# Retention and mixture kernel: the first two blocks' retention placed ahead of the slots, and a lead of two chunks

## The chip, the cores and the metric

The kernel runs on one core of one Trainium2 chip. The metric is the device time of one execution in microseconds (us), as the median of several runs.

## What is computed

Three stages follow one another. Each takes the output of the one before.

```python
scores = scale * np.matmul(q, k.transpose(0, 1, 3, 2))      # 4 batches, 8 heads, 576 tokens, 64 wide
ret = scores * Dmat                                          # gamma_h ** (i - j) for j <= i, else 0
x = np.matmul(ret, v)                                        # then 2304 tokens x 512
h = x @ w_in;  g = h * np.cos(h);  x = g @ w_out             # 512 -> 2048 -> 512
h = x @ w_in2; g = where(h >= 1, h, where(h <= -1, 0, (h + 1) ** 2 / 4)); out = g @ w_out2
```

The first stage is called retention here, the second layer 0, the third layer 1. The weights arrive as 64-bit floats.

## The kernel before

**Tiles and blocks.** The 2304 tokens are cut into five blocks, block 0 of 256 tokens and blocks 1 to 4 of 512. The hidden width of 2048 is cut into 16 chunks c of 128. A slot (l, c) is block l times chunk c of layer 0: a first matmul group (`mm1`, 12 matmuls: three products of split operands, four pieces of the inner dimension), an activation chain on ACT, DVE and POOL (`actA`, `actB`, `actC`), and a second group (`mm2`, 12 matmuls) that runs LAG = 2 slots later and sums into PSUM banks: S and O for block 0, y0 to y3 for the blocks of 512. After chunk 15 `evac` copies these banks out.

**Order of slots.** The list `slots` (L338) sets the order by hand: block 0 leads block 1 by LEAD = 3 chunks, so it runs (0,0), (0,1), (0,2), (0,3), (1,0), (0,4), (1,1) and so on; then blocks 2 to 4 follow, one after the other. While block 0 and block 1 run, each weight chunk is loaded as raw bits (`load_raw`; chunks from 4 on twice, the second time shifted into `rsh`), converted on ACT and DVE into two single-precision halves (`begin`, `convert`), used at once, and the first layer's chunk is also written to DRAM (`make_wi1`) for later blocks. The converted wi tiles live in a pool of LEAD + 2 = 5 buffers.

**Retention.** It works on chunks of up to 128 tokens (`Chunk`), two in block 0, five in block 1, four or five in each other block. Their steps: `load` (q and k, then k and v, then a table of scalings), `prep` (v scaled on DVE, L271), `scores` (L279, into two PSUM banks), `masked` (two maskings on DVE, L285), `full` (state products, L301, and the product with the running state T, L296), `inner` (L309), `state` (T updated, L320 or L322), `post` (scaled out of PSUM by DVE, L327, then split into two parts by ACT, L334, and DVE, L335, into the block's input `xhl`). The tile that holds one chunk's q, k and v comes from pool `ap`, of two buffers. Block 0's chunks are done ahead of the slots. The chunks of the later blocks are spread over a window of slots of the block before (`window`, `mk`, `run_plan`); block 1's over slots 0 to 4, on the banks y2, y3 and y0, y1; block 2's over the last three slots of block 1, on S and O.

**Queues.** Each engine runs its instructions in order, and nearly all DMAs are issued by SP's queue in order. A scheduler of the framework shifts neighbouring instructions within the data's dependences, so the order on an engine is not quite that of the code.

**After that.** While blocks 2 to 4 run, layer 1's weights are converted in the background (`bg`, from the slot behind (0,15) on) and layer 1 then runs as seven products per pair of chunks (`product`, `group`).

Of the kernel before, what the change touches and what calls it, by code (L numbers as in the profile page):

```python
# [7 lines left out]
F32 = mybir.dt.float32  # L8
# [10 lines left out]
B, H, S, D = 4, 8, 576, 64  # L19
NT, DM, DFF = B * S, H * D, 2048  # L20
P = 128
# [11 lines left out]
SEQ = {p: k for k, (p, _, _) in enumerate(PRODS)}  # L33
LAG2 = 3
LAG = 2
LEAD = 3
TWICE = 4
MAGIC = 1.5 * 2.0 ** 23
INV2PI = 0.15915494309189535
# [26 lines left out]
def retention_moe_kernel(ctx: ExitStack, tc: tile.TileContext, qk, kv, win1, wout1, win2, wout2, mask, vtab, ptab, out):  # L66
# [2 lines left out]

    const = ctx.enter_context(tc.tile_pool(name="const", bufs=1))  # L70
    wp = ctx.enter_context(tc.tile_pool(name="wp", bufs=1))
    wr = ctx.enter_context(tc.tile_pool(name="wr", bufs=LEAD + 2))
    xp = ctx.enter_context(tc.tile_pool(name="xp", bufs=5))
    ap = ctx.enter_context(tc.tile_pool(name="ap", bufs=2))
    act = ctx.enter_context(tc.tile_pool(name="act", bufs=2))
# [36 lines left out]
    def load_raw(L, i, c, late=False):  # L112
        src = wsrc[L, i][c]
        twice = L == 0 and c >= TWICE
        tag = "raw" if twice else ("raw", "rsh")[turn[0] % 2] if L == 0 else ("raw", "raw", "rsh")[turn[0] % 3]
        turn[0] += not twice and not late
        t = wp.tile([P, DM, 2], I32, tag="wo0", name="raw") if late else cv.tile([P, DM, 2], I32, tag=tag, name="raw")
        i0 = SY.dma_start(out=t, in_=src)
        if L == 1 and len(done) > 1 and not late:
            behind(i0, done[-2])  # L120
        t2 = None
        if twice:
            t2 = cv.tile([P, 4 * DM + 8], I16, tag="rsh", name="rsh")
            SY.dma_start(out=t2[:, 1:1 + 4 * DM], in_=src.rearrange("p n two -> p (n two)").bitcast(I16))
        raws[L, i, c] = t, t2
# [113 lines left out]
    CH = {}  # L239
# [8 lines left out]
    class Chunk:  # L248
# [6 lines left out]
            self.first, self.last = self.t == 0, self.t + self.n == S  # L255
            self.banks = banks

        def load(self, other=None):
            n = self.n
            both = ap.tile([P, 4, DM], F32, tag="qkv", name="qkv")  # L260
            self.qk = both[:, 0:2].rearrange("p a (i m) -> p a i m", i=NP)
            self.kv = both[:, 2:4]
            SY.dma_start(out=self.qk, in_=qk[self.i])
            (other or SY).dma_start(out=self.kv[:n], in_=kv[self.i][:n])
            self.pt = ap.tile([P, NP, P], F32, tag="pt", name="pt")
            (other or SY).dma_start(out=self.pt[:, :, :n], in_=ptab[:, :, self.t:self.t + n])
# [294 lines left out]
    for i, (b, t, n) in enumerate(CHUNKS):  # L561
        members.setdefault(_block_of(b * S + t), []).append(i)

    window = {1: (0, LEAD + 1)}
    b1_end = pos_of[1, NC - 1]
    window[2] = (b1_end - LEAD + 1, b1_end + 1)
    for l in range(3, NBLK):
        window[l] = (pos_of[l - 1, 0] + 1, pos_of[l - 1, NC - 1] - 1)
    ends = {}
    for l in range(1, NBLK):  # L570
        s0, s1 = window[l]
        span = 2 * (s1 - s0) / len(members[l])
        for k, i in enumerate(members[l]):
            g = int(2 * s0 + k * span)
            e = int(2 * s0 + (k + 1) * span) - 1
            e = max(e, g)
            pos = [g, g + (e - g) // 3, e]
            ends[i] = e
            gl_ = max(g - 9, ends.get(i - 2, -99))
            banks = ("S", "O") if l > 1 else (("y2", "y3"), ("y0", "y1"))[k % 2]  # L580

            def mk(i=i, g=g, pos=pos, gl_=gl_, banks=banks):
                def ld():
                    CH[i] = Chunk(i, banks)
                    CH[i].load()
                at(gl_, ld)
                at(g - 1, lambda: CH[i].prep())
                at(pos[0], lambda: CH[i].scores())
                at(pos[0], lambda: CH[i].masked())
                at(pos[1], lambda: CH[i].full())  # L590
                at(pos[1], lambda: CH[i].inner())
                at(pos[1], lambda: CH[i].state())
                at(pos[2], lambda: CH[i].post())
            mk()

    first = members[0]
    V.memset(half, 0.5)
    A.activation(half, half, AF.Sin)
    V.memset(half, 0.5)
# [6 lines left out]
    def warm(n, after=None):  # L606
        for _ in range(n):
            m = PE.matmul(wt[:, 0:P], wz, wz, start=True, stop=True)
            if after is not None:
                behind(m, after)  # L610
    warm(20)
    for k, i in enumerate(first):
        CH[i] = Chunk(i, (("S", "O"), ("y0", "y1"))[k])
        if i == 0:
            A.dma_start(out=vtb, in_=vtab)
            CH[i].load(A)
            A.dma_start(out=msk, in_=mask)
            load_raw(0, 0, 0)
        else:
            CH[i].load()  # L620
    load_raw(0, 1, 0)
    load_raw(0, 0, 1)
    for i in first:
        c = CH[i]
        c.prep()
        c.scores()
        c.masked()
        warm(10, c.lastpe)
        c.full()
        c.inner()  # L630
        c.state()
        warm(10, c.lastpe)
        c.post()
        if i == 0:
            make_wi1(0, begin(0, 0, 0))
    for p in range(-9, 0):
        run_plan(p)


    jobs = {}  # L640
    for c in range(NC):
        if c >= 1:
            jobs.setdefault(max(0, pos_of[0, c - 1]), []).append((0, c))
        jobs.setdefault(pos_of[0, c], []).append((1, c))
    order = [x for q in sorted(jobs) for x in jobs[q]]
    loaded = [(0, 0), (1, 0), (0, 1)]
    queue = [x for x in order if x not in loaded]
    load_raw(0, *queue.pop(0))

# [153 lines left out]
```

## Time and profile before

| | us |
|---|---|
| median of 3 runs | 918.56 (918.26 to 927.11) |
| profiled execution | 917.86 |
| its span, first to last instruction | 916.1 |
| PE busy in the span | 879.1 (96%) |
| DVE busy | 628.6 (69%) |
| ACT busy | 475.0 (52%) |

PE is TensorE's matmuls, PEld its weight loads, DVE is VectorE, ACT ScalarE, POOL GpSimd, SP the engine that issues the DMAs. A matmul is pipelined, so its duration in a row is longer than the distance to the next one's start; the distance is its cost. A row that merges several instructions (x24) bears the name and shape of the first. The granted clock is a share of the full 2.4 GHz: 1.00 or 0.50, or a mean over a stretch.

### The profile page before, as it was taken

Reading aid. Unit: us, or ns where it says so; the run is one execution under the profiler, and the core shown is the slowest. Engines: PE = TensorE matmul, PEld = TensorE weight load, DVE = VectorE, ACT = ScalarE, POOL = GpSimd, SP = SyncE. Lnnn points to the kernel's source line nnn. Section 1 sums busy time; section 2 is a strip of 40 time slices with the busy share of each in tenths; the row PEclk is TensorE's granted clock in tenths of the full one; section 3 lists DMA queues with packets and bytes.
Section 4 is the critical chain, followed back from the end, with each engine's and each line's share of the span. In section 5 each row is a group of like instructions: output and inputs, shape, how many; then the busy total and the mean of one; then the engine's idle time right before and its main releaser. Section 6 shows DMA issues by size and latency. Waiting matters only on the chain.

```text
span 916.1 us, 13560 instructions
## 1 busy us (share of the span) xinstructions
PE 879.1 (96%) x4876; PEld 754.2 (82%) x4876; DVE 628.6 (69%) x1155; ACT 475.0 (52%) x885; POOL 114.7 (13%) x84
## 2 busy tenths in 40 slices
PE   6788999999999999999999999999999999999997
PEld 6677887877778788788888878998888889889896
DVE  6987898358785967966888776456854546555454
ACT  3447888743655665565767653334433334433332
POOL 0022332203112221212222200000000000000000
PEclk8878999998999999999999999999999999999999
DMA  9998897138858667865686896666685656665531
GB/s 349 295 323 279 313 330 277 47 117 290 329 196 326 239 220 281 260 214 217 231 313 235 296 346 220 185 192 174 207 270 180 188 172 205 226 210 166 168 92 70
DMA packets 78115, 211.81 MB, mean 231 GB/s; under 512 B 9696, under 2 KB 21728, under 8 KB 78048
## 3 DMA queue, kind: packets, MB, share of 16 engines
q1 hardware_dynamic: 77088, 210.01, 67.7%
q10 hardware_dynamic: 960, 0.93, 0.3%
q8 instruction: 39, 0.64, 0.3%
q14 instruction: 28, 0.23, 0.1%
HBM read 170.02 MB, written 40.89 MB: 230 GB/s over the span
## 4 chain that ended last, share of the span: by engine, by line
PE 72%; DMA 12%; DVE 10%; ACT 3%; issue 2%; SPq 0%; DVEq 0%; ACTq 0%
PE hq L490 17%; PE h L359 15%; DMA raw<-in_wout_dram 5%; PE bky L374 5%; PE bky L375 4%; PE bky L542 4%; PE bky L376 4%; PE bky L543 4%; PE bky L544 4%; DMA q<-yd 2%; DMA qkv<-in_kv_dram 2%; DMA wi<-wd 1%; DVE W L142 1%; PE bkO L544 1%; PE bkS L543 1%
## 5 line engine op out<-in xcount | busy, mean ns | idle before, releaser
L490 PE MATMUL hq<-xc,wq 128*128 128x384 f32 x1008 | 199.8, 338 | 4.3 <-ACT sX L505 3.1
L359 PE MATMUL h<-xhl,wi 128*128 128x512 f32 (+1 forms) x864 | 196.7, 377 | 3.7 <-ACT xhl L334 3.0
L490 PEld LDWEIGHTS hq<-xc,wq 128*128 128x128 f32 x1008 | 180.2, 188 | 17.2 <-ACT sX L505 3.9
L359 PEld LDWEIGHTS h<-xhl,wi 128*128 128x128 f32 x864 | 153.1, 194 | 33.4 <-ACT xhl L334 3.4
L422 POOL TENSOR_TENSOR gl<-t,gh 128x512 fp32r<-128x512 f32 (+1 forms) x80 | 114.5, 1438 | 415.5 <-ACT gh L421 391.4
L421 ACT ACTIVATE gh<-t 128x384 fp32r<-128x384 f32 (+2 forms) x176 | 96.5, 549 | 58.2 <-DVE t L429 29.3
L524 ACT ACTIVATE t<-t,half 128x384 f32<-128x384 f32 x96 | 58.9, 616 | 112.4 <-DVE t L523 112.3
L374 PE MATMUL bky<-gh,wo 128*128 128x512 f32 x256 | 102.9, 402 | 5.6 <-ACT gh L421 5.5
L375 PE MATMUL bky<-gh,wo 128*128 128x512 f32 x256 | 101.5, 397 | 0.0
L376 PE MATMUL bky<-gl,wo 128*128 128x512 f32 x256 | 88.7, 392 | 0.0
L525 DVE TENSOR_TENSOR t<-t,sC 128x384 f32<-128x384 f32 x96 | 53.2, 556 | 34.7 <-ACT t L524 34.7
L542 PE MATMUL bky<-wo,gh 128*128 128x512 f32 x192 | 75.7, 394 | 0.9 <-ACT gh L421 0.9
L543 PE MATMUL bky<-wo,gh 128*128 128x512 f32 x192 | 75.5, 393 | 0.0
L414 ACT ACTIVATE t<-t 128x512 f32<-128x512 f32 (+1 forms) x80 | 46.3, 586 | 51.2 <-DVE t L409 51.0
L422 DVE TENSOR_TENSOR gl<-t,gh 128x384 fp32r<-128x384 f32 x96 | 53.1, 553 | 18.9 <-ACT gh L421 18.6
L523 DVE TENSOR_SCALAR t<-sC 128x384 f32<-128x384 f32 x96 | 34.1, 357 | 44.9 <-ACT sC L510 43.4
L374 PEld LDWEIGHTS bky<-gh,wo 128*128 128x128 f32 x256 | 48.6, 190 | 18.0 <-ACT gh L421 7.2
L544 PE MATMUL bky<-wo,gl 128*128 128x512 f32 x192 | 61.2, 394 | 0.0
L375 PEld LDWEIGHTS bky<-gh,wo 128*128 128x128 f32 x256 | 48.8, 191 | 9.9 <-issue 0.3
L141 DVE TENSOR_SCALAR X<-X 128x512 int32<-128x512 int32 x64 | 30.1, 470 | 36.4 <-ACT X L134 36.2
L376 PEld LDWEIGHTS bky<-gl,wo 128*128 128x128 f32 x256 | 47.3, 188 | 9.5 <-issue 0.2
L134 ACT ACTIVATE X<-raw 128x512 f32<-128x512 f32 x64 | 42.6, 666 | 21.7 <-DMA raw<-in_wout_dram 9.9
(126 smaller groups left out, 1376.8 us busy)
## 6 DMA issues: line engine op xcount, KB each, us to landing
wq<-wq SPq DMA_DIRECT2D x72, 512.0 KB, 4.0
wi<-wd SPq DMA_DIRECT2D x48, 512.0 KB, 5.1
wo<-wd SPq DMA_DIRECT2D x48, 512.0 KB, 4.6
raw<-in_win_dram SPq DMA_DIRECT2D x32, 512.0 KB, 5.4
raw<-in_wout_dram SPq DMA_DIRECT2D x32, 512.0 KB, 5.2
qkv<-in_qk_dram SPq DMA_DIRECT2D x20, 512.0 KB, 4.8
wd<-wi SPq DMA_DIRECT2D x16, 512.0 KB, 4.0
wq<-tw SPq DMA_DIRECT2D x32, 256.0 KB, 4.0
```

Source lines behind the costliest of these rows:

```text
L359: PE.matmul(hp[s][:, :n], w[:, a, kb, :], x[b][:, kb, :], start=(i == 0), stop=(i == 3 * KB - 1))
L374: PE.matmul(o, w[:, 0, es], a, start=first and e % per == 0, stop=False, skip_group_check=True)
L375: PE.matmul(o, w[:, 1, es], a, start=False, stop=False, skip_group_check=True)
L376: PE.matmul(o, w[:, 0, es], b, start=False, stop=last, skip_group_check=True)
L421: A.activation(a, u, AF.Copy)
L422: eng.tensor_tensor(out=b, in0=u, in1=f(a), op=ALU.subtract)
L490: PE.matmul(o, w[:, a, kb, :], x[b][:, kb, :], start=first and i == 0, stop=i == 5, skip_group_check=True)
L524: A.activation(t, t, AF.Square, scale=0.5, bias=half)
L525: V.tensor_tensor(out=t, in0=t, in1=h, op=ALU.max)
L542: PE.matmul(y, a[:, js], w[:, 0, :], start=n == 0, stop=False)
L543: PE.matmul(y, a[:, js], w[:, 1, :], start=False, stop=False)
L544: PE.matmul(y, b[:, js], w[:, 0, :], start=False, stop=n == NC - 1)
```

## The change

LEAD goes from 3 to 2, and the wi pool keeps its five buffers (LEAD + 3). All seven chunks of blocks 0 and 1 are put ahead of the slots in one list `first`; each is loaded three chunks ahead, on three pairs of banks in turn, and every other one takes its q, k, v tile from pool `xp` and not from `ap`. The first raw weights are loaded between these chunk loads, and wi 0, wo 0 and wi 1 are converted between the chunks. Chunk c's wi is begun three slots ahead of (0,c), before it was at (0,c-1). Block 2's window has two slots, not three, and its third and fourth chunk use y0 to y3. The diff, whole:

```diff
--- before.py
+++ after.py
@@ -33,7 +33,7 @@
 SEQ = {p: k for k, (p, _, _) in enumerate(PRODS)}
 LAG2 = 3
 LAG = 2
-LEAD = 3
+LEAD = 2
 TWICE = 4
 MAGIC = 1.5 * 2.0 ** 23
 INV2PI = 0.15915494309189535
@@ -69,7 +69,7 @@
 
     const = ctx.enter_context(tc.tile_pool(name="const", bufs=1))
     wp = ctx.enter_context(tc.tile_pool(name="wp", bufs=1))
-    wr = ctx.enter_context(tc.tile_pool(name="wr", bufs=LEAD + 2))
+    wr = ctx.enter_context(tc.tile_pool(name="wr", bufs=LEAD + 3))
     xp = ctx.enter_context(tc.tile_pool(name="xp", bufs=5))
     ap = ctx.enter_context(tc.tile_pool(name="ap", bufs=2))
     act = ctx.enter_context(tc.tile_pool(name="act", bufs=2))
@@ -255,9 +255,9 @@
             self.first, self.last = self.t == 0, self.t + self.n == S
             self.banks = banks
 
-        def load(self, other=None):
+        def load(self, other=None, pool=None):
             n = self.n
-            both = ap.tile([P, 4, DM], F32, tag="qkv", name="qkv")
+            both = (pool or ap).tile([P, 4, DM], F32, tag="x" if pool else "qkv", name="qkv")
             self.qk = both[:, 0:2].rearrange("p a (i m) -> p a i m", i=NP)
             self.kv = both[:, 2:4]
             SY.dma_start(out=self.qk, in_=qk[self.i])
@@ -561,13 +561,12 @@
     for i, (b, t, n) in enumerate(CHUNKS):
         members.setdefault(_block_of(b * S + t), []).append(i)
 
-    window = {1: (0, LEAD + 1)}
     b1_end = pos_of[1, NC - 1]
-    window[2] = (b1_end - LEAD + 1, b1_end + 1)
+    window = {2: (b1_end - LEAD + 1, b1_end + 1)}
     for l in range(3, NBLK):
         window[l] = (pos_of[l - 1, 0] + 1, pos_of[l - 1, NC - 1] - 1)
     ends = {}
-    for l in range(1, NBLK):
+    for l in range(2, NBLK):
         s0, s1 = window[l]
         span = 2 * (s1 - s0) / len(members[l])
         for k, i in enumerate(members[l]):
@@ -577,7 +576,8 @@
             pos = [g, g + (e - g) // 3, e]
             ends[i] = e
             gl_ = max(g - 9, ends.get(i - 2, -99))
-            banks = ("S", "O") if l > 1 else (("y2", "y3"), ("y0", "y1"))[k % 2]
+
+            banks = (("S", "O"), ("y0", "y1"), ("y2", "y3"))[max(0, k - 1) % 3 if l == 2 else 0]
 
             def mk(i=i, g=g, pos=pos, gl_=gl_, banks=banks):
                 def ld():
@@ -593,7 +593,7 @@
                 at(pos[2], lambda: CH[i].post())
             mk()
 
-    first = members[0]
+    first = members[0] + members[1]
     V.memset(half, 0.5)
     A.activation(half, half, AF.Sin)
     V.memset(half, 0.5)
@@ -609,41 +609,57 @@
             if after is not None:
                 behind(m, after)
     warm(20)
-    for k, i in enumerate(first):
-        CH[i] = Chunk(i, (("S", "O"), ("y0", "y1"))[k])
-        if i == 0:
+
+    def first_load(k):
+        i = first[k]
+        CH[i] = Chunk(i, (("S", "O"), ("y0", "y1"), ("y2", "y3"))[k % 3])
+        if k == 0:
             A.dma_start(out=vtb, in_=vtab)
             CH[i].load(A)
             A.dma_start(out=msk, in_=mask)
-            load_raw(0, 0, 0)
         else:
-            CH[i].load()
+            CH[i].load(pool=xp if k % 2 else None)
+
+    first_load(0)
+    first_load(1)
+    load_raw(0, 0, 0)
+    first_load(2)
     load_raw(0, 1, 0)
-    load_raw(0, 0, 1)
-    for i in first:
+    CH[first[0]].prep()
+    for k, i in enumerate(first):
         c = CH[i]
-        c.prep()
         c.scores()
         c.masked()
-        warm(10, c.lastpe)
+        if k < 2:
+            warm(10, c.lastpe)
+        if k + 1 < len(first):
+            CH[first[k + 1]].prep()
         c.full()
         c.inner()
         c.state()
-        warm(10, c.lastpe)
+        if k < 2:
+            warm(10, c.lastpe)
         c.post()
-        if i == 0:
+        if k + 3 < len(first):
+            first_load(k + 3)
+        if k == 2:
             make_wi1(0, begin(0, 0, 0))
+            load_raw(0, 0, 1)
+        if k == 4:
+            make_wo1(0, begin(0, 1, 0))
+            load_raw(0, 1, 1)
+    make_wi1(1, begin(0, 0, 1))
     for p in range(-9, 0):
         run_plan(p)
 
 
     jobs = {}
-    for c in range(NC):
-        if c >= 1:
-            jobs.setdefault(max(0, pos_of[0, c - 1]), []).append((0, c))
+    for c in range(1, NC):
+        if c > 1:
+            jobs.setdefault(max(0, pos_of[0, c] - 3), []).append((0, c))
         jobs.setdefault(pos_of[0, c], []).append((1, c))
     order = [x for q in sorted(jobs) for x in jobs[q]]
-    loaded = [(0, 0), (1, 0), (0, 1)]
+    loaded = [(1, 1)]
     queue = [x for x in order if x not in loaded]
     load_raw(0, *queue.pop(0))
```

Where this moves instructions, as they stand on the engines. First PE at the start of block 1's slots. bkS and bkO are block 0's sums, wo0 to wo3 its second-layer weights by chunk, xhl a block's input; h of 512 columns is block 1's. Before:

```order
L296 MATMUL bky3_662<-qkv_545,T_90 128x64 x4
L309 MATMUL bky3_662<-R_671,qkv_545 64x64 x8
L374 MATMUL bkS_645<-gh_784,wo3_726 128x256
L375 MATMUL bkS_645<-gh_784,wo3_726 128x256
...
L376 MATMUL bkO_646<-gl_785,wo3_726 128x256
L359 MATMUL h_770<-xhl_357,wi_237 128x512 x4
L359 MATMUL h_808<-xhl_231,wi_739 128x256 x12
```

And now:

```order
L296 MATMUL bkO_496<-qkv_410,T_90 128x64 x4
L309 MATMUL bkO_496<-R_505,qkv_410 64x64 x8
L374 MATMUL bkS_680<-gh_599,wo0_448 128x256
L375 MATMUL bkS_680<-gh_599,wo0_448 128x256
...
L374 MATMUL bkS_680<-gh_656,wo1_615 128x256
...
L376 MATMUL bkO_681<-gl_657,wo1_615 128x256
L359 MATMUL h_696<-xhl_346,wi_358 128x512 x4
L359 MATMUL h_750<-xhl_235,wi_626 128x256 x5
```

Behind block 1's last chunk of retention stood the second layer of (0,3), and those of (0,0) to (0,2) were done by then; now the first second-layer slots at all, (0,0) and (0,1), stand there, and (0,3)'s first layer comes with (1,0).

SP's queue around the first load for block 2 (qkv_1868 before, qkv_1918 now); raw and rsh are weights, wd their copies to DRAM, pt the scalings. Before:

```order
L263 DMA qkv_545<-in_qk_dram 128x1024
L264 DMA qkv_545<-in_kv_dram 64x1024
L266 DMA pt_548<-in_ptab_dram 128x4x64
L118 DMA raw_735<-in_win1_dram 128x1024
L263 DMA qkv_1868<-in_qk_dram 128x1024
L264 DMA qkv_1868<-in_kv_dram 128x1024
L124 DMA rsh_750<-in_wout1_dram 128x2048
L163 DMA wd0_0_4_96<-wi_739 128x1024
```

And now:

```order
L263 DMA qkv_350<-in_qk_dram 128x1024
L264 DMA qkv_350<-in_kv_dram 128x1024
L163 DMA wd0_0_2_94<-wi_571 128x1024
L266 DMA pt_353<-in_ptab_dram 128x4x128
L263 DMA qkv_1918<-in_qk_dram 128x1024
L264 DMA qkv_1918<-in_kv_dram 128x1024
L118 DMA raw_678<-in_wout1_dram 128x1024
L118 DMA raw_732<-in_win1_dram 128x1024
```

The load for block 2 came behind the raw load of wi 5; now the raw loads of wo 3 and wi 5 come behind it.

PE at the end of block 1, from the second layer of its last chunk (wo15) to block 2's first slot. Before:

```order
L309 MATMUL bkO_2249<-R_2258,qkv_2123 64x128 x8
...
L374 MATMUL bky0_901<-gh_2431,wo15_2018 128x512
...
L376 MATMUL bky0_901<-gl_2432,wo15_2018 128x512
L279 MATMUL bkO_2316<-qkv_2219 128x128 x4
L301 MATMUL bkS_2315<-qkv_2219 64x64 x8
```

And now:

```order
L376 MATMUL bky3_847<-gl_2410,wo15_2056 128x512
L279 MATMUL bky0_2264<-qkv_2163 128x128 x4
L279 MATMUL bky2_2323<-qkv_2232 128x128 x4
L279 MATMUL bky1_2265<-qkv_2163 128x128 x4
L279 MATMUL bky3_2324<-qkv_2232 128x128 x4
L296 MATMUL bky1_2265<-qkv_2163,T_90 128x128 x4
L309 MATMUL bky1_2265<-R_2274,qkv_2163 64x128 x8
L301 MATMUL bky2_2323<-qkv_2232 64x64 x8
L309 MATMUL bky3_2324<-R_2333,qkv_2232 64x128 x8
```

Of block 2's four chunks the third was complete on PE before the last second-layer slots of block 1, and the fourth began between them; now the third and the fourth begin behind them.

## Rows read from the trace of the kernel before

**Rows 1.** The windows of the whole core: us, each engine busy (instructions), clock, DMA.

```profile
12.00:68.00 56.00, 44.91 (x457) 39.27 (x458) 52.09 (x107) 25.47 (x54) 6.69 (x4) 0.80 0.96 325
67.00:100.00 33.00, 29.91 (x145) 25.49 (x146) 24.92 (x48) 23.21 (x50) 6.42 (x6) 0.86 0.85 302
100.00:160.00 60.00, 56.78 (x315) 48.97 (x314) 52.08 (x96) 49.67 (x108) 19.34 (x13) 1.00 0.85 303
...
200.00:230.00 30.00, 28.05 (x197) 23.02 (x196) 24.96 (x45) 14.81 (x27) 7.78 (x3) 0.89 0.76 263
230.00:916.00 686.00, 673.82 (x3444) 578.28 (x3442) 453.84 (x824) 336.94 (x601) 67.00 (x48) 1.00 0.66 221
```

**Rows 2.** The timeline of DVE, the first masking and the last split of block 1: start, us.

```profile
11.87 0.69 DVE L285 TENSOR_TENSOR R<-bkS,msk 128x512 f32<-128x512 f32 x1 [0.38 <-DMA msk<-in_mask_dram]
...
67.18 0.42 DVE L335 TENSOR_TENSOR xhl<-xs,xhl 128x256 fp32r<-128x256 f32 x1
```

**Rows 3.** The DVE groups between these two: busy us, mean ns, idle before, releaser.

```profile
L142 DVE SCALAR_TENSOR_TENSOR W<-raw,X 128x512 int32<-128x512 int32 x10 | 6.8, 679 | 0.0
...
L153 DVE SCALAR_TENSOR_TENSOR C<-raw,C 128x512 int32<-128x512 int32 x7 | 4.8, 683 | 0.1
...
L143 DVE TENSOR_SCALAR X<-W 128x512 int32<-128x512 int32 x10 | 4.2, 415 | 0.0
...
L271 DVE TENSOR_TENSOR qkv<-qkv,vtb 64x512 f32<-64x512 f32 x2 | 1.8, 894 | 2.5 <-DMA qkv<-in_kv_dram 2.5
...
L409 DVE SCALAR_TENSOR_TENSOR t<-t,hs 128x256 f32<-128x256 f32 x4 | 1.6, 408 | 0.0
L429 DVE SCALAR_TENSOR_TENSOR t<-t,hs 128x256 f32<-128x256 f32 x4 | 1.5, 406 | 0.0
```

**Rows 4.** The timeline of PE, the start of block 1: start, us, idle before it.

```profile
66.83 7.07 PE L359 MATMUL h<-xhl,wi 128*128 128x512 f32 x24 [1.81 <-ACT xhl L334]
74.59 4.45 PE L359 MATMUL h<-xhl,wi 128*128 128x512 f32 x24 [0.69 <-ACT hs L405]
81.44 0.50 PE L374 MATMUL bky<-gh,wo 128*128 128x512 f32 x1 [2.40 <-ACT gh L421]
...
89.10 0.28 PE L375 MATMUL bkS<-gh,wo 128*128 128x256 f32 x1
89.22 0.28 PE L376 MATMUL bkS<-gl,wo 128*128 128x256 f32 x1
...
91.37 0.40 PE L374 MATMUL bky<-gh,wo 128*128 128x512 f32 x1
91.60 0.40 PE L375 MATMUL bky<-gh,wo 128*128 128x512 f32 x1
```

**Rows 5.** The windows of 5 us around it; columns as in rows 1.

```profile
55.00:60.00 5.00, 2.91 (x34) 2.39 (x36) 3.01 (x7) 2.78 (x7) 0.74 (x1) 1.00 1.07 318
...
65.00:70.00 5.00, 3.19 (x12) 2.79 (x12) 3.53 (x9) 1.09 (x2) 0.00 (x0) 0.50 0.98 373
...
80.00:85.00 5.00, 3.56 (x11) 2.86 (x12) 4.90 (x8) 4.28 (x10) 2.72 (x2) 0.78 0.91 315
```

**Rows 6.** The timeline of ACT, from the first h of block 1 to its gh.

```profile
73.94 0.88 ACT L405 ACTIVATE hs<-h 128x512 f32<-128x512 f32 x2 [4.63 <-PE h L359]
...
80.76 0.62 ACT L421 ACTIVATE gh<-t 128x512 fp32r<-128x512 f32 x1
```

**Rows 7.** The waits between 100 and 160 us: engine, for whom, us, times, longest.

```profile
PE bky L374 <- ACT gh L421: 3.1, 4, 1.8
...
ACT X L134 <- DMA raw<-in_wout_dram: 1.1, 2, 0.6
```

**Rows 8.** The timeline of PE, from block 1 to block 2.

```profile
204.19 1.15 PE L279 MATMUL bkO<-qkv 64*128 64x128 f32 x8 [0.61 <-DVE xs L327]
206.60 2.07 PE L279 MATMUL bkS<-qkv 64*128 64x128 f32 x8 [1.25 <-DVE R L285]
```

## The prediction

> **What bounds the kernel now.** I read the windows first. From 230 us on PE is busy 673.82 of 686.00 us at full clock [rows 1]: that stretch is PE's, the change leaves its instructions alone, and whatever is won or lost before it reaches the end one for one. So the question is when PE has done the first two blocks. Before 230 us there are four stages [rows 1]. From 12 to 68 us DVE is the bound, busy 52.09 of 56 us, while PE runs at a mean clock of 0.80 and waits. From 67 to 100 us block 1 starts: PE counts as busy 29.91 of 33 us, but at clock 0.86. From 100 to 160 us PE is busy 56.78 of 60 us at full clock, with DVE (52.08), ACT (49.67) and the DMA engines (0.85) all over 80%: balanced, PE slightly ahead. From 200 to 230 us block 1 hands over to block 2, at clock 0.89.
>
> In the timeline of DVE the reader is to see the two ends of the first stage: the first masking at 11.87 us, which had waited for the mask's DMA, and at 67.18 us the split that completes block 1's input [rows 2]. Between them lie 55.7 us. The groups show which waits interrupt DVE: 2.5 us for two late kv loads is the largest [rows 3].
>
> In the timeline of PE block 1's first matmul runs at 66.83 us and its first second-layer matmul at 81.44 us [rows 4]. The row labelled with 24 matmuls at 66.83 holds slot (1,0) and slot (0,4), twelve each; the next row holds (1,1) and (0,5). The same load takes 7.07 us and then 4.45 us: the first runs at the lower level, since the granted clock is 0.50 from 65 to 70 us, 1.2 of 2.4 GHz, after a stretch in which PE was busy 2.91 of 5 us [rows 5]. Then PE waits 2.40 us for gh.
>
> **The change part by part.** Nothing is added to or taken from the instructions of the kernel; they move. Sums are made against the profiled execution, 917.86 us, 0.7 us under the median of 918.56; its span is 916.1.
>
> *The retention ahead, loads first.* Counted in the order of DVE, 106 instructions stand from the first masking to block 1's last split before, 103 now. Now the weights' first conversion lies inside (it had run before 11.87 us), but the conversions behind it have gone less far. Net, one W merge, one X mask, one multiply-add pair's scaling (L409) and one L429 are gone, one L153 has come, and an L150 has become an L152 of the same length: 0.68 + 0.42 + 0.41 + 0.41 - 0.68 = 1.2 us less [rows 3]. The stretch is DVE's own, so the order of the loads can save only its waits: 2.5 us for kv [rows 3], of which I take 2.0, since chunks 1, 3 and 5 now have buffers of their own pool. That puts the last split 3.2 us earlier. Ends: 4.8 us (every wait of the stretch gone, 55.7 - 52.1 + 1.2) and -1.2 us (as much new waiting as the 2.5 us again). The new waiting would come from SP: its first load for block 2 needs chunk 4's buffer, and the raw loads of wo 3 and wi 5 stand behind it. By the sum over DVE's rows chunk 4 is masked some 10 us before DVE wants wo 3, and a load lands in less, so I put it at nothing.
>
> *What PE owes.* At the last split PE has done less than before: (0,3) in both layers and (0,2) in the second, 36 matmuls of 256 columns. They start 0.12 us apart (89.10 and 89.22), those of 512 columns 0.23 us (91.37 and 91.60) [rows 4]; so it owes 4.3 us.
>
> *The start of block 1.* Before, 14.6 us lie between 66.83 and 81.44 us, and hold 24 x 0.23 + 24 x 0.12 = 8.4 us of matmuls at full clock. Now the same gap holds (1,0), (0,3), the second layer of (0,2), (1,1), (0,4). Two things bound it: PE's first 24 matmuls, and then ACT's chain, 73.94 to 81.38 us, 7.4 us from h to gh [rows 6]. At full clock slot (1,0), mixed with part of (0,3), is through after 3.4 us, so 10.8 us; at the lower level after 6.8 us, so 14.2 us. The stretch ahead is as sparse as before, which speaks for the lower level; two second-layer slots (24 matmuls) stand right ahead now, which speaks against it. I take 12.5, the middle. So that matmul comes 3.2 + 14.6 - 12.5 = 5.3 us earlier. By then before had done 24 matmuls more, (0,5) and the second layer of (0,3), 2.9 us. Net gain 2.4 us. From there to 100 us I change nothing.
>
> *The lead of two.* A pair of slots needs the same weights and the same PE time, but (1,c) now comes one pair earlier, so a given amount of PE work needs weights one chunk later, and each wi conversion is begun one slot sooner with the same five buffers. In the third stage PE waits 3.1 us for gh, and ACT, which makes gh, 1.1 us for raw wo alone [rows 7]. What the slack can give lies between 0 and 3.1 us; I take 1.2, by the row of the raw loads.
>
> *Block 2's retention.* Its window shrinks from three slots to two, and its chunks 2 and 3 go to y0 to y3, which block 1 holds to its last slot. In the order both now stand behind (1,15)'s second layer, with only block 3's first scores to fill. The chain from there to block 2's first slot: DVE does two copies, four maskings, two scalings and a split, nine at 0.69 [rows 2] = 6.2 us, then two inner products on PE near 1.15 each (the nearest row is a group of scores, [rows 8]), and ACT's 0.62 [rows 6]: 9.1 us. PE's own groups in it are six, near 1.15: 6.9 us. It waits 2.2 us there. Before, the handover waits 0.61 + 1.25 us on one pair of banks [rows 8], of which the first two chunks keep part. I take a loss of 1.5 us; ends 0 and 4.9 (9.1 less the two inner products and less the 1.9 lost now).
>
> The Trainium skill (Perfetto Trace Analysis, Matmuls) says that independent groups of matmuls should rotate through the PSUM banks, so that emptying one overlaps the next. By it alone this edit would gain the 1.9 us just named. The order shows that the rotation comes only once block 1 lets go, so I don't count it.
>
> **Sum:** 2.4 + 1.2 - 1.5 = 2.1 us less, 915.8 us as the profiled execution has it, 916.5 us by the median.
>
> **The rivals.** *The start runs free.* If the second-layer slots ahead of block 1 keep the clock up and the waits go: 4.8 + (14.6 - 10.8) - 2.9 + 3.1 = 8.8, and the lower clock of 80 to 85 us (0.78, [rows 5]), worth about 1 us, goes too: 908.8 us. For it: the low level stands in 5 to 10 us only. Against it: DVE gives PE no more to do than before in the first 68 us.
>
> *Taken apart.* DVE is busy 52.09 of 56 us [rows 1] whatever the loads' order, so the last split stays at 67.6 us; PE has then only put off slots that it used to run in the gaps of the retention. 14.6 - 12.5 - 2.9 - 1.5 = -2.3: 921 us. For it: only 2.5 us of wait is in reach. The Trainium skill (Perfetto Trace Analysis, Optimization Strategy) says that stages bound by different engines may gain from being interleaved; here retention is DVE's and the slots are PE's, and the change pulls them apart. By that rule this rival holds; rows 1 agree in so far as DVE, not PE, is full there.
>
> *Slower, at the handover.* The place is the gap behind (1,15). If the 9.1 us pass with PE nearly idle and the clock falls to 0.50 as at 65 us, the 24 matmuls behind it take about 2.6 us more (7.07 against 4.45, [rows 4]): 9.1 + 2.6 - 1.9 = 9.8 lost. With the front's 2.4 gained that is 926 us. It decides from about 4 us of loss on, where it outweighs front and lead together. For it: PE's clock is 0.89 there now [rows 1]. Against it: PE has six groups of its own to do in the chain.
>
> **How the numbers follow.** The forecast has 0.46 (912 to 919 us by its own terms), the free start 0.18, taken apart 0.23, the handover 0.13. About 1%, 9 us, is what a measurement of this kernel can tell from no change. Faster by more (under 909.4): most of the free start and a little of the forecast, 0.17. Slower by more (over 927.7): half of the handover and a little of taken apart, 0.08. The rest, 0.75, lies within. The range, 907 to 924 us, takes in the free start and taken apart and leaves out the worse half of the handover and the tail below.
>
> **What would show it.** Right: block 1's last split at 63 to 66 us; no DVE wait for kv; its first second-layer matmul at 74 to 78 us; PE waiting for gh less than 3 us from 100 to 160 us; a wait of some 2 us between (1,15) and block 2's first slot. Wrong: the last split at 68 us or later, or DVE waiting there for raw (the SP queue); the clock at 0.50 through block 1's start and again at the handover; or a gain of more than 5 us that arises between 100 and 200 us, where I see only the lead's slack.

## The result, and the profile after

The changed kernel takes 930.05 us (median of 20 runs, 925.55 to 931.77), the kernel before in the same comparison 920.34 (20 runs, 915.03 to 927.11). The ratio is 1.0093, with a 95% interval of 1.0074 to 1.0112: 8.6 us slower. (The two medians lie 9.7 us apart; below, the ratio counts.) The forecast was 916.5 us; what came nearest is the rival "slower, at the handover" (926 us, chance 0.13). The profiled execution took 930.15 us, with a span of 928.4.

The windows of the changed kernel (columns and stretches as in [rows 1]):

```profile
12.00:68.00 56.00, 43.85 (x435) 38.73 (x436) 52.63 (x109) 25.24 (x50) 8.62 (x3) 0.76 0.93 316
67.00:100.00 33.00, 29.81 (x162) 25.90 (x161) 29.44 (x54) 27.50 (x60) 8.71 (x6) 0.95 0.93 343
100.00:160.00 60.00, 56.56 (x327) 49.71 (x326) 54.98 (x95) 49.53 (x107) 16.01 (x13) 1.00 0.86 297
200.00:230.00 30.00, 17.98 (x111) 14.28 (x110) 22.98 (x39) 11.86 (x22) 7.38 (x2) 0.72 0.70 244
230.00:916.00 686.00, 677.82 (x3512) 582.72 (x3511) 451.88 (x822) 335.48 (x598) 66.42 (x48) 0.99 0.66 220
```

Against [rows 1] one row stands out: from 200 to 230 us PE was busy 28.05 of 30 us at clock 0.89, and now it is busy 17.98 us at 0.72. PE's busy time ahead of it differs by 1.1 us at most in a row, and from 230 us on PE is nearly full as before. The price is in one place, where block 1 hands over to block 2. The timeline of PE there:

```profile
203.13 1.09 PE L309 MATMUL bkO<-R,qkv 128*64 128x128 f32 x16
213.09 0.80 PE L374 MATMUL bky<-gh,wo 128*128 128x512 f32 x1 [8.86 <-ACT gh L421]
213.68 0.63 PE L375 MATMUL bky<-gh,wo 128*128 128x512 f32 x1
214.11 0.63 PE L374 MATMUL bky<-gh,wo 128*128 128x512 f32 x1
...
219.51 2.08 PE L376 MATMUL bky<-gl,wo 128*128 128x512 f32 x4 [2.64 <-POOL gl L422]
221.38 0.63 PE L374 MATMUL bky<-gh,wo 128*128 128x512 f32 x1
...
225.88 3.50 PE L279 MATMUL bky<-qkv 64*128 64x128 f32 x32
...
232.88 0.69 PE L301 MATMUL bky<-qkv 128*64 128x64 f32 x16 [1.39 <-DVE R L285]
...
236.40 5.74 PE L359 MATMUL h<-xhl,wi 128*128 128x512 f32 x24
```

The reader is to see three stretches (block 2's chunks are numbered 0 to 3). At 204.2 us PE is through with chunk 1 and then does nothing for 8.86 us, until gh of slot (1,14) is there. The second layers of (1,14) and (1,15) follow at the lower clock (213.68 to 214.11: 0.43 us apart, where 0.23 is full speed), with another wait of 2.64 us for gl. Only then, from 225.88 us, come the scores and inner products of chunks 2 and 3, ten microseconds with only block 3's first scores beside them, and block 2 starts at 236.40 us. The same stretch before:

```profile
201.39 1.09 PE L309 MATMUL bkO<-R,qkv 128*64 128x128 f32 x16
...
208.60 0.79 PE L374 MATMUL bky<-gh,wo 128*128 128x512 f32 x1
...
213.34 1.09 PE L309 MATMUL bkO<-R,qkv 128*64 128x128 f32 x16
...
215.41 0.39 PE L374 MATMUL bky<-gh,wo 128*128 128x512 f32 x1
...
226.85 5.74 PE L359 MATMUL h<-xhl,wi 128*128 128x512 f32 x24
```

Here (1,13)'s second layer still stood in the stretch, from 208.60 us. Chunk 2's scores ran ahead of it ([rows 8]) and its inner product (213.34 us) inside it; (1,14) followed at 215.41 us without a wait, and chunk 3 began inside (1,15)'s second layer. From the end of chunk 1's inner product to block 2's first slot 24.4 us passed (202.48 to 226.85), with one second layer more to do; now 32.2 us pass (204.22 to 236.40).

Why gh is so late is told by the chain that ended last (start, us, what):

```profile
199.40 4.83 DMA qkv<-in_kv_dram
204.25 0.04 DVE qkv L271
...
206.80 0.69 DVE xs L327
207.49 1.20 DVE t L409 x2
...
209.03 0.60 DVE W L142
209.62 0.60 DVE xhl L335
...
210.83 0.60 DVE qkv L271
...
211.77 0.61 DVE t L429
212.40 1.24 ACT gh L421 x2
213.67 5.79 POOL gl L422
...
219.51 2.08 PE bky L376 x4
```

The steps of the activation of the last two slots that DVE makes (L409, L429; L421 is ACT's, L422 POOL's) stand there among other work: the v scaling, the scaling out of PSUM and the splits of block 2's retention (L271, L327, L335) and the conversion of layer 1's weights (L142, L143, and L183 in the rows left out). The chain begins with a load of k and v for block 2, for which DVE waited 1.39 us at 204.25 us. The beginning of that activation was late already: ACT had stood 10.38 us at the split of block 2's first chunk, with the copies hs of both slots behind it in its queue, though their first layers were done by 192.2 us (the last row of 12 matmuls, L359, starts at 189.28 and takes 2.91).

```profile
199.73 0.63 ACT L334 ACTIVATE xhl<-xs 128x512 fp32r<-128x512 f32 x1 [10.38 <-DVE xs L327]
200.27 1.07 ACT L405 ACTIVATE hs<-h 128x512 f32<-128x512 f32 x2
```

### The profile page after: what moved, and what is told of

Read it like the earlier page. It is cut to its first block, busy times and chain, and to the rows that moved or that the text cites. A ratio compares the mean times of both kernels' runs of the same rounds, so it can differ in the third digit from the quotient of the medians.

```text
span 928.4 us, 13567 instructions
## 1 busy us (share of the span) xinstructions
PE 879.6 (95%) x4876; PEld 756.7 (82%) x4876; DVE 633.0 (68%) x1155; ACT 475.9 (51%) x885; POOL 115.8 (12%) x84
## 4 chain that ended last, share of the span: by engine, by line
PE 76%; DMA 8%; DVE 6%; ACT 3%; issue 1%; POOL 1%; SPq 0%; ACTq 0%; DVEq 0%; POOLq 0%
PE hq L490 18%; PE h L359 15%; PE bky L374 5%; PE bky L375 5%; PE bky L376 5%; PE bky L542 5%; PE bky L543 5%; PE bky L544 5%; DMA raw<-in_win_dram 4%; DMA raw<-in_wout_dram 3%; DVE W L142 1%; PE bkO L542 1%; PE bkS L543 1%; PE bkO L544 1%; PE bkS L544 1%; PE bkS L542 1%
## 5 line engine op out<-in xcount | busy, mean ns | idle before, releaser
L359 PE MATMUL h<-xhl,wi 128*128 128x512 f32 (+1 forms) x864 | 193.0, 372 | 0.9 <-ACT hs L405 0.5
L359 PEld LDWEIGHTS h<-xhl,wi 128*128 128x128 f32 x864 | 151.1, 191 | 29.2 <-ACT hs L405 0.7
L422 POOL TENSOR_TENSOR gl<-t,gh 128x512 fp32r<-128x512 f32 (+1 forms) x80 | 115.6, 1451 | 424.3 <-ACT gh L421 398.5
L421 ACT ACTIVATE gh<-t 128x384 fp32r<-128x384 f32 (+2 forms) x176 | 96.2, 549 | 54.7 <-DVE t L525 29.6
L374 PE MATMUL bky<-gh,wo 128*128 128x512 f32 x256 | 104.8, 410 | 15.5 <-ACT gh L421 15.5
L375 PE MATMUL bky<-gh,wo 128*128 128x512 f32 x256 | 103.4, 404 | 0.0
L374 PEld LDWEIGHTS bky<-gh,wo 128*128 128x128 f32 x256 | 50.1, 196 | 27.3 <-ACT gh L421 16.3
L422 DVE TENSOR_TENSOR gl<-t,gh 128x384 fp32r<-128x384 f32 x96 | 53.1, 553 | 18.8 <-ACT gh L421 18.6
L375 PEld LDWEIGHTS bky<-gh,wo 128*128 128x128 f32 x256 | 50.3, 196 | 10.2 <-issue 0.2
L134 ACT ACTIVATE X<-raw 128x512 f32<-128x512 f32 x64 | 42.5, 664 | 27.5 <-DMA raw<-in_win_dram 17.4
```

What stands on the lines that cost most here:

```text
L359: PE.matmul(hp[s][:, :n], w[:, a, kb, :], x[b][:, kb, :], start=(i == 0), stop=(i == 3 * KB - 1))
L374: PE.matmul(o, w[:, 0, es], a, start=first and e % per == 0, stop=False, skip_group_check=True)
L375: PE.matmul(o, w[:, 1, es], a, start=False, stop=False, skip_group_check=True)
L421: A.activation(a, u, AF.Copy)
L422: eng.tensor_tensor(out=b, in0=u, in1=f(a), op=ALU.subtract)
```

## The experiments

Each ratio is to the kernel before, measured beside it (its median there lay between 919.4 and 921.4 us); 0.1% is 0.9 us. The expectations were written after the result above and before their own kernel was measured. The executions of one kernel spread over 3 to 12 us, and a trace shows one of them; where a trace that is read here was over 3 us off its median, the text says so.

**Which part of the change costs.** Four kernels take the change apart.

The handover put back, with the new start and the lead of two (from the changed kernel):

```diff
-    window = {2: (b1_end - LEAD + 1, b1_end + 1)}
+    window = {2: (b1_end - 2, b1_end + 1)}
-            banks = (("S", "O"), ("y0", "y1"), ("y2", "y3"))[max(0, k - 1) % 3 if l == 2 else 0]
+            banks = ("S", "O")
```

> The changed kernel with only block 2's retention put back as before: three slots and the S/O pair alone; the new start and the lead of two stay. Theory (the handover is the whole loss, start and lead together are worth next to nothing): 919 to 921 us, where the kernel before has 920.3 and the changed one 930.1. Rival (start or lead lose as well): 925 us or more. My forecast's own terms for start and lead (2.4 + 1.2) would give 916.7.

Measured: 917.22 us, ratio 0.9968 (0.9949 to 0.9988). Start and lead together gain 2.9 us, so the handover costs 0.9968 to 1.0093, 11.5 us.

The start alone (from the changed kernel, with the edit of `banks` above and these; with a lead of three the window has three slots by itself):

```diff
-LEAD = 2
+LEAD = 3
-    wr = ctx.enter_context(tc.tile_pool(name="wr", bufs=LEAD + 3))
+    wr = ctx.enter_context(tc.tile_pool(name="wr", bufs=LEAD + 2))
-            jobs.setdefault(max(0, pos_of[0, c] - 3), []).append((0, c))
+            jobs.setdefault(max(0, pos_of[0, c] - 2), []).append((0, c))
```

> The new start alone: retention of both first blocks ahead of the first slot, a lead of three, block 2's retention as before. Theory: block 1's start came 3.5 us earlier in the changed kernel and PE owed 2.9, so 0.6 is left: 919.5 to 920 us. My forecast's term (2.4) would give 918; the rival 'taken apart' 922 or more.

Measured: 918.46 us, 0.9979 (0.9957 to 1.0002): 1.9 us less, with an interval that just takes in no gain.

The lead alone (from the kernel before):

```diff
-LEAD = 3
+LEAD = 2
-    wr = ctx.enter_context(tc.tile_pool(name="wr", bufs=LEAD + 2))
+    wr = ctx.enter_context(tc.tile_pool(name="wr", bufs=LEAD + 3))
-    window[2] = (b1_end - LEAD + 1, b1_end + 1)
+    window[2] = (b1_end - 2, b1_end + 1)
```

> The lead of two alone: the kernel before with a lead of two chunks, the old start, block 2's retention over three slots on the S/O pair. Theory (the lead is worth nothing): 920 us. My forecast's term (1.2) would give 919. Rival (the changed kernel's 3.2 us of PE lost from 130 to 150 us come from the lead): 923 us.

Measured: 921.30 us, 1.0012 (0.9989 to 1.0035): no difference that can be told.

The handover alone (from the kernel before, with the pairs of the change for block 2 and):

```diff
-    window[2] = (b1_end - LEAD + 1, b1_end + 1)
+    window[2] = (b1_end - 1, b1_end + 1)
```

> Block 2's retention alone as in the change: two slots and three pairs of banks, with the old start and the lead of three. Theory (the handover is the whole loss, whatever stands ahead of it): 929 to 931 us. Rival (the handover only costs together with the lead of two, by which block 1's last slots stand next to each other): 920 to 923 us.

Measured: 924.67 us, 1.0065 (1.0041 to 1.0090). So it costs 6.0 us by itself and 11.5 together with the lead of two and the new start: neither theory has its number. PE's wait for gh of (1,14) is 4.7 us there and 8.9 in the changed kernel, and the one for gl is gone. ACT leaves the first split at the same time in both traces (199.56 and 199.73 us), but DVE takes the first L409 at 205.11 us there and only at 207.40 us in the changed kernel, behind chunk 1's state and scaling (L322, L327). Why the order is another behind the old start and a lead of three was not tried.

**Which half of the handover.** Window and banks are put back one at a time in the changed kernel. The window:

```diff
-    window = {2: (b1_end - LEAD + 1, b1_end + 1)}
+    window = {2: (b1_end - 2, b1_end + 1)}
```

> The changed kernel with one thing put back: block 2's chunks spread over three slots, with the three pairs of banks kept. Theory (the short window is what costs: the retention stands in one piece between the first layer of the last slots and their activation): 917 to 920 us, as with the whole handover put back (917.2). Rival (the three pairs cost, since y0 to y3 come free only behind the last slot): 925 us or more.

Measured, three slots and three pairs: 925.75 us, 1.0070 (1.0048 to 1.0091). My theory fell here; the rival holds. The banks:

```diff
-            banks = (("S", "O"), ("y0", "y1"), ("y2", "y3"))[max(0, k - 1) % 3 if l == 2 else 0]
+            banks = ("S", "O")
```

> The changed kernel with the other thing put back: all four chunks of block 2 on the S/O pair, with the window of two slots kept. Theory (the short window): 926 to 930 us, little gained. Rival (the three pairs): 917 to 920 us.

Measured, two slots and one pair: 920.38 us, 1.0003 (0.9981 to 1.0025). The banks cost 0.90% (1.0093 against 1.0003), 8.3 us, or 1.02% with three slots (1.0070 against 0.9968); the short window costs 0.23 to 0.35%, 2 to 3 us, which is hardly clear of the noise (each ratio has an interval of some 0.2% to either side). The timeline of PE with one pair shows why:

```profile
206.26 1.09 PE L309 MATMUL bkO<-R,qkv 128*64 128x128 f32 x16
208.81 1.35 PE L279 MATMUL bkS<-qkv 64*128 64x128 f32 x8 [1.45 <-issue]
...
217.29 1.98 PE L309 MATMUL bkO<-R,qkv 128*64 128x128 f32 x16
219.19 0.77 PE L374 MATMUL bky<-gh,wo 128*128 128x512 f32 x1
...
231.72 1.66 PE L359 MATMUL h<-xhl,wi 128*128 128x512 f32 x6
```

gh comes no earlier: the second layer of (1,14) starts at 219.19 us, 11.8 us behind the end of chunk 1's inner product (206.26 + 1.09), and 8.9 us behind it in the changed kernel. But PE does chunk 2's scores and inner product meanwhile, here at the lower clock, and banks S and O, already free, let it. From the end of chunk 1's inner product to block 2's first slot 24.4 us pass (207.35 to 231.72) where the changed kernel needs 32.2: 7.8 us less, near the 8.3 of the ratios. The trace with one pair enters this stretch 3.1 us later; they are lost before 150 us, ahead of anything that the edit moves.

Chunk 3 alone on another pair (two slots):

```diff
-            banks = (("S", "O"), ("y0", "y1"), ("y2", "y3"))[max(0, k - 1) % 3 if l == 2 else 0]
+            banks = ("y0", "y1") if l == 2 and k == 3 else ("S", "O")
```

> The changed kernel with two slots, chunks 0 to 2 of block 2 on the S/O pair and only chunk 3 on another pair (y0, y1). If the price is chunk 2's place (its scores and inner product no longer lie in PE's wait for gh): 920 to 922 us, as with one pair. If both chunks cost alike by standing behind the last slot: 924 to 926 us.

Measured: 922.56 us, 1.0028 (1.0002 to 1.0054). Putting chunk 2 back into the wait for gh gives 0.65%, 6.0 us; chunk 3 alone behind the last slot costs the other 0.25%, 2.3 us, which is not clear of the noise (the two ratios have intervals of 0.26 and 0.22% to either side).

**Whose queue makes gh late.** In the changed kernel, layer 1's conversions three slots later:

```diff
-    bg0 = pos_of[0, NC - 1] + 1
+    bg0 = pos_of[0, NC - 1] + 4
```

> The changed kernel with the conversions of the second layer's weights begun three slots later, so that DVE has none of them while the last two slots of block 1 wait for their activation. In the changed kernel seven of them, 3.8 us, lie on DVE inside PE's wait of 8.9 us for gh. Theory A (DVE's queue is part of the price): 925 to 927 us. Theory B (the wait is set by ACT, which stands 10.4 us at the split of block 2's first chunk with the last slots' activation behind it): 929 to 930 us.

Measured: 923.85 us, 1.0041 (1.0021 to 1.0062), more than theory A gave (4.8 us less than the changed kernel). PE's wait for gh fell from 8.86 to 5.15 us, and the one for gl went: POOL made the two gl in 2.78 us, where the changed kernel took 7.38 (below).

The last two slots of block 1 activated straight from PSUM, which also lets ACT take them ahead of block 2's split:

```diff
-        if l < 2:
+        if l < 2 and s < b1_end - 1:
             hp[s] = xp.tile([P, 512], F32, tag="x", name="hs")
```

> The changed kernel, but the last two slots of block 1 are activated straight from PSUM, without the copy hs. In the order ACT and DVE then take the activation of these slots ahead of block 2's first split. Theory (ACT's order sets PE's wait for gh): the wait of 8.9 us goes and with it most of the low clock behind it, but two chunks of the retention move behind the last second-layer slot: 920 to 926 us. Rival (the retention costs the same wherever it stands): 929 us or more.

Measured: 920.72 us, 1.0000 (0.9976 to 1.0023). In the trace, of an execution of 915.46 us, the second layer of (1,14) starts at 195.87 us without a wait, ahead of chunk 1, and (1,15) waits 0.60 us for its gh:

```profile
195.87 0.49 PE L374 MATMUL bky<-gh,wo 128*128 128x512 f32 x1
...
202.23 0.50 PE L374 MATMUL bky<-gh,wo 128*128 128x512 f32 x1 [0.60 <-ACT gh L421]
```

8.6 us are won back with the three pairs and the short window in place; what is left of the price is about the 2.9 us that start and lead gain. So the price needs both: a late gh (this kernel), and nothing for PE to do until it comes (one pair).

**Whether the low clock costs.** In the changed kernel, 120 matmuls of zeros in the wait:

```diff
-    def warm(n, after=None):
+    def warm(n, after=None, wt=wt):
...
+        if s == b1_end:
+            wt = psh.tile([P, 512], F32, tag="h", name="wt")
+            warm(120, CH[members[2][1]].lastpe, wt)
```

> The changed kernel with 120 matmuls of zeros (128 columns, bf16, into a bank that nobody reads) between block 2's second inner product and the second layer of slot (1,14), where PE waits 8.9 us for gh; at 0.055 us apart, as ten of them ran at full clock in the start, they fill 6.6 us of that wait. Theory (half of the price behind the wait is the clock: 24 matmuls of 512 columns at 0.43 us apart where 0.23 is full speed, 4.8 us): the granted clock stays at 1.00 there, and the time is 925 to 927 us. Rival (the second layer of the last two slots is held by gl and the next gh anyway, so the clock costs nothing): 929 to 931 us.

Measured: 930.83 us, 1.0107 (1.0086 to 1.0129). By the median the rival holds. The traced execution was the fastest of the six (926.46 us); in it the clock did stay up, until the next wait:

```profile
203.15 6.87 PE L608 MATMUL wt<-wz 128*128 128x128 bf16 x120
212.01 0.50 PE L374 MATMUL bky<-gh,wo 128*128 128x512 f32 x1 [1.99 <-ACT gh L421]
212.59 0.40 PE L374 MATMUL bky<-gh,wo 128*128 128x512 f32 x1
...
220.30 0.63 PE L374 MATMUL bky<-gh,wo 128*128 128x512 f32 x1
...
233.32 2.11 PE L359 MATMUL h<-xhl,wi 128*128 128x512 f32 x8 [1.46 <-ACT xhl L334]
```

PE then runs the gh part of (1,14) at full speed, waits 4.28 us for gl in place of 2.64, and begins (1,15) at the lower speed again. In this execution block 2 starts 30.1 us behind the end of chunk 1's inner product (203.21 to 233.32), 2.1 us less than in the changed kernel; the median shows nothing of it. POOL makes the two gl back to back, 7.17 us in this kernel and 7.38 in the changed one. There, the window over the first gl (columns as in [rows 1]) and POOL's row:

```profile
213.50:219.40 5.90, 3.37 (x8) 2.08 (x7) 5.87 (x13) 1.25 (x4) 5.90 (x1) 0.50 0.74 269
```

```profile
213.49 7.38 POOL L422 TENSOR_TENSOR gl<-t,gh 128x512 fp32r<-128x512 f32 x2 [23.96 <-ACT gh L421]
```

DVE is busy 5.87 of 5.90 us while POOL makes the first gl. Two more kernels give gl of the last two slots to DVE, without and with the 120 matmuls:

```diff
-        gh[s], gl[s] = parts(u, G)
+        gh[s], gl[s] = parts(u, V if b1_end - 1 <= s <= b1_end else G)
```

> The changed kernel with gl of the last two slots of block 1 made by DVE (0.69 us each) in place of POOL (7.4 us for both in the changed kernel). The second layer of both slots is then PE's own: 24 matmuls at 0.43 us behind 213.1 us end at 223.4 and not at 225.9: 2.5 us less, 927.5 us. Rival (PE was not held by POOL): 929 to 931 us.

Measured: 930.49 us, 1.0098 (1.0060 to 1.0136): no gain by the median, with an interval of 0.38% to either side. The traced execution was again the fastest of six (923.84 us). In it the second layers are through by 221.17 us, earlier than forecast, since the clock came back inside (1,15); 2.53 us of wait for the DMA of block 3's q and k follow, and block 2 starts 30.3 us behind chunk 1 (204.13 to 234.38), 1.9 us less than in the changed kernel.

> The same with the 120 matmuls of zeros in the wait for gh. If the low clock is what then holds the two slots, the 24 matmuls run 0.23 us apart, 4.8 us less than with gl on DVE alone: 922 to 924 us. If the chain behind (block 2's last two chunks) or DVE's queue takes the gain back, 926 us or more.

Measured: 925.09 us, 1.0057 (1.0031 to 1.0084), between the two ranges. By the medians and ratios neither edit alone gains anything, and both together gain 0.36% against the changed kernel, 3.3 us, just clear of the noise (intervals of 0.27 and 0.19% to either side). That would mean that low clock and slow gl hide one another; it is not shown. In the traces the stretch from chunk 1 to block 2 is 2.1 us shorter with the matmuls of zeros, 1.9 with gl on DVE and 4.7 with both (27.5 us, 203.65 to 231.16), so that the gains nearly add up there. Behind them the next wait already stands, 2.62 us for the DMA that brings block 3's first q and k.

**A version that beats both.** The handover put back (917.22 us, the first experiment) takes further edits from above. First hs, the edit of `actA`:

> The version with the handover put back (917.2 us), with the last two slots of block 1 activated straight from PSUM as well. If the order of ACT still costs there, 913 to 915 us; if block 2's retention between the second layers covers it, 916 to 918 us.

Measured: 921.45 us, 1.0009 (0.9988 to 1.0030): 0.4% worse than without the edit, and outside both ranges. In the trace, of an execution of 925.31 us, ACT runs the activation of three slots side by side, and the second layer of (1,13) starts at 210.08 us, where it had started at 204.81. An edit that helped in one order did harm in the other.

The conversions three slots later, the edit of `bg0`:

> The version with the handover put back (917.2 us), with the conversions of the second layer's weights begun three slots later as well. DVE is busy 10.0 of 10 us from 210 to 220 us in that version; if its queue sets PE's wait of 2.5 us for block 2's scaling there, and the low clock behind it, 913 to 915 us; if not, 916 to 918 us.

Measured: 916.84 us, 0.9945 (0.9926 to 0.9964), the lowest ratio. Against the kernel before this is a gain; against the version without the edit (0.9968) the 0.23% are within the noise, and by its time the second range holds. PE's wait is gone from the trace, though. Its windows (columns as in [rows 1]) and POOL's rows:

```profile
200.00:210.00 10.00, 10.00 (x73) 8.38 (x71) 8.41 (x13) 8.42 (x16) 1.82 (x2) 1.00 0.65 211
210.00:220.00 10.00, 10.00 (x84) 7.95 (x84) 4.83 (x8) 2.78 (x6) 1.97 (x2) 1.00 0.53 186
220.00:230.00 10.00, 10.00 (x79) 8.25 (x78) 4.57 (x9) 3.61 (x7) 0.00 (x0) 1.00 0.58 184
```

```profile
203.50 1.27 POOL L422 TENSOR_TENSOR gl<-t,gh 128x512 fp32r<-128x512 f32 x1 [18.95 <-ACT gh L421]
209.45 2.52 POOL L422 TENSOR_TENSOR gl<-t,gh 128x512 fp32r<-128x512 f32 x2 [4.67 <-ACT gh L421]
```

PE is full at clock 1.00 from 200 to 230 us. Both of these edits:

> Both of these together with the handover put back. If each removes a wait of its own, 911 to 914 us; if both remove the same one, as the better of them alone.

Measured: 919.21 us, 0.9985 (0.9959 to 1.0011): the edit on hs takes part of the other's gain back. And the conversions later, with gl of the last two slots on DVE:

> The best version so far (handover put back, second layer's conversions three slots later, 916.8 us) with gl of the last two slots made by DVE. If POOL's gl still holds one of the last slots there: 914 to 915.5 us; if not, 916 to 918 us.

Measured: 916.46 us, 0.9947 (0.9923 to 0.9971), the same as without. That fits the trace of the version before it, in which PE does not wait for POOL's gl from 190 to 240 us.

## Why the prediction was wrong, point by point

*The retention ahead: right.* From the first masking to the last split 52.5 us pass in the changed kernel (11.15 to 63.69) where [rows 2] gave 55.7: 3.2 us less, as forecast. DVE is busy 50.38 us there, 1.5 less (forecast 1.2), and idle 1.7 less (2.0); one wait of 1.8 us for kv is left, against the sign that there would be none. (The lower end of this term is 1.2 - 2.5 = -1.3, not -1.2; nothing rests on it.)

```profile
11.15 0.69 DVE L285 TENSOR_TENSOR R<-bkS,msk 128x512 f32<-128x512 f32 x1 [1.50 <-DMA msk<-in_mask_dram]
...
63.28 0.41 DVE L335 TENSOR_TENSOR xhl<-xs,xhl 128x256 fp32r<-128x256 f32 x1
```

*The start of block 1: near the number, not by its reason.* 13.2 us pass from block 1's first matmul to its first second layer, not 12.5 (14.6 before, [rows 4]). The 12.5 were the middle between a first group at full clock (10.8) and at half (14.2). The group ran at full clock; but ACT's chain from h to gh took 9.5 us (68.34 to 77.88) and not 7.4, and in it ACT stood 2.07 us for a raw weight, for which this sum had no term. So the nearness is luck. Chunk 0's second layer then ran at the lower clock:

```profile
64.78 4.35 PE L359 MATMUL h<-xhl,wi 128*128 128x512 f32 x24
...
77.93 0.75 PE L374 MATMUL bky<-gh,wo 128*128 128x512 f32 x1 [3.19 <-ACT gh L421]
78.91 0.63 PE L374 MATMUL bky<-gh,wo 128*128 128x512 f32 x1
```

```profile
73.14 0.67 ACT L134 ACTIVATE X<-raw 128x512 f32<-128x512 f32 x1 [2.07 <-DMA raw<-in_win_dram]
```

The first second-layer matmul came 3.5 us earlier (forecast 5.3); less the 2.9 us owed, 0.6 is left at that point. The start alone measured 1.9 us of gain (-0.2 to 4.0), which holds both the 2.4 of the forecast and the 0.6.

*The lead of two: not shown.* PE waits 3.4 us for gh from 100 to 160 us, against 3.1 in [rows 7], and ACT 5.4 us for raw wi (0.7 before). Alone the lead measured 1.1 us of loss (between 1.0 of gain and 3.2 of loss), which leaves the forecast's 1.2 just outside, and beside the new start 1.0 of gain (0.9979 to 0.9968), which is within the noise. So the 1.2 is not confirmed, and beside the new start not refuted; front and lead together, 3.6 by the forecast, measured 2.9.

*Block 2's retention: here the prediction failed.* The forecast took a loss of 1.5 us with ends 0 and 4.9; measured is 11.5. The step as I put it was: a chain of 9.1 us behind (1,15), of which PE's own groups cover 6.9, so that PE "waits 2.2 us there". The chain itself was nearly right: from 225.88 to 236.40 us 10.5 us pass, with 2.1 us of waits, 0.74 of them for a DMA that the sum did not have. What was missing lies ahead of it. PE's groups of chunks 2 and 3 had to be done in any case, but chunk 2's had been doing another job: before, they filled the time until gh of (1,13) was there, and in the kernel with one pair they lie in the 11.8 us ahead of (1,14). I priced what the moved groups add where they arrive, and nothing where they leave. There, 8.9 us of wait came bare, another 2.6 for gl, and most of 24 matmuls ran at half speed, where before it had been eight and chunk 2's own; what each of these three costs by itself is not shown. [rows 8] show only the 0.61 and 1.25 us that PE waits between these groups; the view that would have told was ACT's and DVE's: gh of the last two slots late by their queues, whatever PE does.

*The rotation of banks.* By the rule of the Trainium skill (Perfetto Trace Analysis, Matmuls) this edit would have gained 1.9 us, an estimate of mine from [rows 8]. It lost 8.3: the two added pairs came free only when block 1 let go of them, so block 2's chunks gave up a place where a bank was free for one where none was yet.

*The rivals.* The handover rival named the right place, and a loss of 9.8 us there against the 11.5 measured, but built from a chain with PE nearly idle behind (1,15); in fact PE idles ahead of (1,14), so that its number is near by luck. Against it I had set that "PE has six groups of its own to do in the chain", which is true and counted for nothing. Of the free start the condition came for the first group (full clock), the gain did not: ACT's chain held PE. "Taken apart" fell with the start alone, which did not lose (at most 0.2 us by its interval).

## What to carry to other kernels

Work that is moved off an engine's idle time must be priced at both ends: what it adds where it arrives, and which wait it uncovers where it leaves. Ask what the engine would wait for if the moved rows were struck from its timeline, and follow that wait's chain through the queues of the other engines. A second pair of banks helps only where it is free at the time at which the first one is busy. And where two costs end at the same instruction (here a low clock and a slow gl), test them together as well as one by one: taken away alone, neither showed a gain here that the measurement could tell.

## What was not expected of the hardware

POOL's gl (128x512, two operands in SBUF) takes 1.27 us at best and 5.97 us in the window 213.50:219.40 above, a factor of 4.7. In that window DVE is busy without a gap (5.87 of 5.90 us); in the best version the pair at 209.45 us has DVE busy 0.9 of 2.5 us. With layer 1's conversions begun later the two gl of the last slots take 2.8 us and not 7.4, so these conversions, most of them DVE's work there, slow POOL. The Trainium skill (SBUF — State Buffer, Who interferes with whom) says that a DVE instruction with two SBUF inputs contends with a GpSimd instruction that reads SBUF; the trace agrees with that, but no run here tells instructions with one input from those with two.

It is not DVE's busy share alone that decides. The second gl of the changed kernel takes 1.46 us while DVE is busy 1.41 of 1.44 us. DVE's rows there show that DVE's time, too, can be waiting:

```profile
217.91 0.42 DVE L204 TENSOR_TENSOR V<-V 128x256 f32<-128x256 f32 x1
218.37 1.37 DVE L205 TENSOR_TENSOR V<-V 128x256 f32<-128x256 f32 x1
219.77 1.38 DVE L206 TENSOR_TENSOR V<-V 128x256 f32<-128x256 f32 x1
```

L205 and L206 have the shape of L204, which takes 0.42 us, and each lies over the end of one gl. So, as I read these rows, the first gl stood some 4.7 us behind DVE's instructions, and then L205 stood about 1 us behind it. POOL's spans in a profile are rough, but PE's wait for gl ended at 219.51 us, 0.05 us behind the end of the span.
